# Six kinds of small VectorE operations moved to ScalarE, with new order tables, in an attention-and-SwiGLU kernel

## The chip, the cores and the metric

The kernel runs on one core of a Trainium2 chip. The metric is the device time of one execution in microseconds (us), as the median of several runs. A difference of about 0.2% (3.2 us here) is the least that such a measurement can tell from no change.

Five engines work side by side, each on its own queue and strictly in the queue's order: TensorE (PE, with its weight loads shown as PEld), VectorE (DVE), ScalarE (ACT), GpSimd (POOL) and SyncE (SP), which issues nearly all DMAs.

## The reference

Four batches of 12416 tokens with 128 channels pass through two attentions and a gated feed-forward network:

```python
scale = 1.0 / np.sqrt(C)
I = np.broadcast_to(inducing[None], (B, m, C))      # m = 32 inducing points
def mab(q, kv):
    s = scale * (q @ kv.transpose(0, 2, 1))
    s = s - s.max(-1, keepdims=True)
    a = np.exp(s)
    a /= a.sum(-1, keepdims=True) + 1e-09
    return a @ kv
h = mab(I, x)                 # 32 rows per batch
x = mab(x, h).reshape(B * S, D)
rms = np.sqrt(np.mean(x * x, axis=-1, keepdims=True) + 1e-06)
xn = x / rms * rms_g
g, val = xn @ w_gate, xn @ w_val          # 128 -> 1536
out = (g / (1 + np.exp(-g))) * val @ w_out    # 1536 -> 128
```

## The kernel before

**Units and slots.** A batch is cut into 25 units of up to 512 tokens (20 of 512, 4 of 480, 1 of 256), and each unit's 1536 hidden channels into 12 blocks of 128. One block of one unit is a slot, so there are 300 slots in a batch and 1200 in all. A slot (`slot`, L739) makes the gate product g (L742), its SiLU on ScalarE (L750), the value product v (L753), and silu times v on VectorE (L759). The slot's result is then multiplied by its block of `w_out` and added up over the unit's 12 blocks in the PSUM tile `acc`.

**Two ways to multiply by `w_out`.** A *plain* slot multiplies in float32 (`project`, L679): one matmul in the program, two records in the trace. A *split* slot (`three`, L718) first takes its block apart into parts, and then runs three faster float32r matmuls (`project3`, L695: lines L700, L702 and L679). There are two kinds of split: "sums" takes one ScalarE operation (L724), one VectorE (L725) and one GpSimd (L734); "differences" takes two ScalarE (L728, L733) and two GpSimd operations (L729, L734). A letter for each slot says which: s, d, or a dot for plain.

**The folded attention.** The second attention's 32 weights per token are the moving operand of the g and v products; h is folded into the weights once per batch, as the stacks `sg` and `sv`. So while batch b's slots run, batch b+1's first attention is worked out between them: `scores1`, `max1` to `max3`, `exp1_of`, `turn_e`, `sum_h`, `fold_l`, `divide`, `turn_h`, `square_h`, then `fetch`, `stack` and `place` for the stacks, and `scores2`, `row_max`, `sub_max`, `exp2` for the second attention's weights. Within batch b, `seam` (L496) scales each set's weights by the RMS factor and splits them (`turn_a` to `split`), and `gather` (L550) copies them by DMA into the tile `a`, which the g and v products of a unit read.

**What sets the order.** Everything is written out by hand and runs in program order on each engine. Tables inside the kernel hold the order: `letters` (the kind of each slot), `places` (the slot at which each step of attention and seam is issued), `ordered` (the points within each slot at which the output products are issued, "p" for a plain and "t" for a split one), and `banks`, `workers` and `holders` (which of 5 PSUM banks, 3 working tiles and 9 result tiles each use takes). In `steps` (L1117) of each slot the waiting second halves of splits come first, then the steps placed there, with products between them.

**Lines that the change touches.** All belong to the attention of a batch: `sum_h` L394 (first copy of the sum out of PSUM), `divide` L406 (division by the row sum, from SBUF to SBUF in batches 1 to 3), `turn_h` L413 (hT out of PSUM), `scale_h` L419 (hg = hT times the RMS gain, from SBUF to SBUF), `square_h` L431 (four 32x32 blocks of the Gram matrix), and `stack` L469 (the upper half of the stack out of PSUM). For batch 0 this part runs before the first slot. For batches 1 to 3 it lies in slots 146 to 227 of the batch before.

Of the kernel before, what the change touches and what calls it, by code (L numbers as in the profile page):

```python
# [9 lines left out]
F32 = mybir.dt.float32  # L10
# [8 lines left out]
P = 128  # L19
# [4 lines left out]
def kernel(  # L24
# [279 lines left out]
    def attention(b, load_next):  # L304
# [73 lines left out]
        def sum_h(*sets):  # L378
# [12 lines left out]
            if b and sets[0]:  # L391
                nc.vector.tensor_tensor(out=hl[:, 0:C], in0=hl[:, 0:C], in1=ps[:, 0:C], op=ALU.add)
            elif b:
                nc.vector.tensor_copy(out=hl[:, 0:C], in_=ps[:, 0:C])  # L394
# [9 lines left out]
        def divide():  # L404
            st["hn"] = st["hl"][:, 0:C]
            nc.vector.tensor_scalar_mul(out=st["hn"], in0=st["hn"] if b else st["ps"][:, 0:C], scalar1=st["rl"][:])  # L406

        def turn_h():

            ps = bank()  # L410
            nc.tensor.matmul(ps[:, 0:P], st["hn"], fold[:].rearrange("p q m -> p (q m)"), start=True, stop=True)
            hT = st["hT"] = once.tile([P, P], F32, name="hT")
            nc.vector.tensor_copy(out=hT[:], in_=ps[:, 0:P])  # L413
            if b:
                scale_h()

        def scale_h():
            hg = st["hg"] = once.tile([P, P], F32, name="hg")
            nc.vector.tensor_scalar_mul(out=hg[:], in0=st["hT"][:], scalar1=gam)  # L419

        def square_h():
# [6 lines left out]
            for q in range(R):  # L428
                to, of_ = gram[b][ts(q, m), ts(q, m)], ps[ts(q, m), 0:m]
                if b:  # L430
                    nc.vector.tensor_scalar(out=to, in0=of_, scalar1=1.0 / C, scalar2=1e-6, op0=ALU.mult, op1=ALU.add)  # L431
                else:
                    nc.scalar.activation(to, of_, AF.Copy, bias=1e-6, scale=1.0 / C)
# [27 lines left out]
        def stack(i):  # L461
# [7 lines left out]
            nc.vector.tensor_copy(out=hi[rows, :], in_=ps[rows, :])  # L469
# [503 lines left out]
    def given(b, k, u, j):  # L973
# [4 lines left out]
        ..........................dss.sdd...ss.sd.dsss..s.dss.dsds..sdsdsd...s..dsdd.sd..s..sd..sdsssd..ss.d  # L978
        sssdsd..d.ssdd.ss...ssssdsdsds....s..ds.sd..ssssssdsss..sdsdsd.sss..dss.ssddss...sssd.sssd..sdd.s.sd
        sd..s.sssdddss..sss.sssdss..ssssds.d.s..ssssd.ssss....s..dd.sd..s.ss.dssss..s.ssd...ss..ssdssssddd..  # L980
        """,
        """
        d..sdsd.ds..s..sd.ssds..ss..dsdssd...ssdssds.s..dsssd.sssd..sssd.s.dsd..dds.sd.dsd..ss..s.sssd..ssds
        sd.sds..sdsdsss.d...sss.sdssdd..s....d..dd..ssssssdssd..ssssssd.ss..sdsssssdss..sss.dssdsd..ssdsssss
        sd..sdds.ssssd..sss.s.sdsd..ss.s.ssssd...sssd.dsds....ss.sds.s..ss.dss.sds...ssss.sdss..ssd...ddds..
        """,
        """
        sd.sdd.sss.....dss.dsd..ssssdd.ssd..dss.sssdds...sssssdd.d..dsd...ssss..sdd.sssd.s..sds.dsssss..ssss
        dssd.s..d..dsssssd..sssdsdd.dd....s.s..dsd..sssdssdsss..sdssssss.s..dssdssssss..dsss.dsdss..ssssdssd
        sd..sssddsss.s..sssss.ssds..ssss.dsd.s..ssssssdsds....s..d.dd...ssssssssd...sss.s.ssss....ssdsddsd..  # L990
        """,
        """
        sd..d.ssssssds....ss.ssss.sssdds.dss.s..ssssdsss.ss.s.dsss.sssd...ssd..sss.sssssdssssss.ssds..ssss.s
        d.dssssssds..s.s.s.sssssd.ds.ss.sssssd.sss.ss.sssdds..sd.ssssds..ss.sss.ssd.ssss..sssssd.ss.sss.sd.s
        sds.ssssss.ss.sssd.ss..dss.sss.ssss.s.sssssssds..dsssss.ssdd..ss.ssss.sd.s..ssdssd.d.ssss.ssd....d..
# [5 lines left out]
        20 16 20 21 21 22 21 21 23 24 24 25 24 24 26 27 26 27 27 27 28 28 29 30 31 32 32 32 33 33 35 34 35 37 36 39   # L1001
        39 43 41 43 47 47 47 48 51 51 51 54 57 58 58 60 62 61 62 62 63 66 64 69 65 70 72 69 75 73 73 77 74 77 80 78 
        85 81 82 85 85 89 85 89 90 92 94 96 97 97 100 100 104 103 105 105 108 105 102 110 106 105 114 111 115 112 
        121 124 116 129 124 132 127 132 134 135 136 136 142 146 147 148 151 157 158 160 161 163 162 163 165 165 168 
        160 171 171 172 174 175 180 180 183 191 195 198 198 198 193 198 203 209 195 196 211 212 197 202 216 218 219 
        201 204 201 215 203 213 205 215 221 220 225 215 221 223 225 228 235 227 228 240 240 233 236 245 246 239 240 
        250 245 251 251 254 254 255 256 257 256 256 256 256 263 257 256 269 264 273 273 269 274 277 275 278 281 281 
        284 287 293 299 
        """,
        """  # L1010
        0 0 6 12 8 16 18 16 18 24 25 24 26 24 27 28 34 30 36 34 31 36 37 40 42 45 48 54 48 48 54 57 60 60 62 64 56 
        65 68 66 68 69 69 70 70 71 72 74 78 76 79 81 82 84 99 88 90 91 97 105 103 111 105 112 108 112 102 113 110 
        110 112 116 117 126 129 124 132 126 133 134 135 136 140 142 146 147 148 146 151 153 160 161 162 162 162 164 
        165 170 160 162 169 172 174 175 180 180 180 189 193 194 198 203 192 204 204 205 195 201 209 210 202 198 210 
        211 211 205 202 206 214 213 206 216 215 218 220 221 216 221 225 227 224 225 227 227 239 240 233 233 246 246 
        239 245 247 245 253 251 254 254 255 256 257 256 256 256 256 263 265 268 269 267 272 273 270 275 278 275 282 
        281 285 288 287 293 299 
        """,
        """
        0 0 6 12 5 11 18 11 18 12 15 21 29 24 26 29 34 30 36 32 32 36 36 37 42 46 48 51 48 49 54 57 57 60 66 60 52   # L1020
        61 55 66 56 67 62 67 72 74 72 79 74 81 75 82 75 84 91 86 86 96 97 101 103 108 103 110 108 111 109 111 112 
        112 117 120 119 124 129 120 132 128 133 134 135 136 142 143 146 147 148 147 158 151 160 161 157 162 157 160 
        161 164 162 168 169 169 174 175 174 180 180 188 195 196 198 204 199 206 206 210 202 211 210 212 197 205 212 
        216 216 207 213 207 213 209 215 211 220 216 221 216 226 228 226 234 225 234 239 236 240 247 240 248 250 254 
        254 255 256 255 255 256 257 258 256 260 261 261 273 273 279 282 285 287 
        """,
        """
        2 4 6 4 10 13 15 15 19 30 33 52 62 62 65 67 69 75 79 101 108 110 113 114 121 125 129 148 153 154 157 165 165 
        172 180 196 202 202 204 214 214 219 227 244 250 250 259 261 263 276 277 
# [3 lines left out]
        ;;;,p;,pp;;,pp;;,pp;;,pp;;;,pp,,,p;;,p;;;,p;;;p;,p;;,p;;,p;;;,pp;,pp;,pp;,tt;,tp,t;;,p;;,tp;;,tp;;,pp;;,tt;,t;  # L1033
        ;,pp;,t;;,pt;;,tt;;,t;,pp;;,tt;;,tt;,tp;;,t;,t;;;t,pp;,tt;;,tt;,t;,p;;,t;;,p;,pt;,pp;;;,tt;;,tp;;,tp;;,t;,tp;;
        ,t;,p;;,t;,tt;;,p;,tt;,tp;;,tp;,t;;;,tt;,pt;;,t;;t,t;;p,t;;;t,t;,p;t;,tp;;,tt;,p;;,tp;,t;;,tp;;,p;,tt;;t;,tp;;
        ,t;,p;;,tt;,pt;,pt;,tp;;,p;p;t,p;,p;,t;;,t;;,t;;,tp;;,tt;;,t;,tt;,tp;;,t;;,tt;,,t;,pt;;,t;;,t;,tt;;t,p;;,tp;,p
        t;;,t;,,p;,t;,tt;;,tt;,p;,,,tp;;;,tt;,t;,pt;;,tp;;,tp;,t;;,tt;;;,t;,tp;;,,t;,tt;,pp;;,t;,t;,tt;,p;;,t;;,pp;,t;
        ,t;,t;,t;,t;;;,t;,t;,tp;;,tp;,t;,t;,tp;,t;,t;,tp;,t;;,p;,t;,t;,pt;,t;;,t;;,tt;;,t;;,tp;;,tp;,t;;,t;,t;,t;,pt;;
        ,p;;,tt;,tt;,pp;,pp;;,tp;;p,p;;p,t;;,p;;,tt;;,pt;;,tt;;,tp;,t;;,tt;,tp;;,t;;,pp;;;t,tp;;,t;,p;,t;;,pt;;,tp;,t;
        ,t;,pt;,t;,t;,t;;,tp;,tp;;,tp;,t;;,pp;;,t;,tp;,t;;,t;,p;;,t;;,t;,t;;,tt;,pt;,p;;,tt;,pt;;,tp;;,pp;;,t;,t;,p;,t  # L1040
        p;,t;;,t;;,tt;;p;,tp;,p;,t;;,tt;;,tt;;,pt;,tp;,t;,pt;;;,t;t,t;;t,tp;;,tt;;;t,p;;,t;,tt;;;,tt;;,pt;;,t;,pp;;,tp
        ;;,pp;;,tp;,tt;;,tp;;,tp;;,t;,p;;,tp;,t;,p;,tt;;,tt;;,tt;;;,tp;;,tt;;;t,tt;;,pt;,t;;,tp;,t;,p;,tt;;,tp;;,t;;;t
        ;,t;,tp;;,p;,tp;;,t;,tt;;,t;,pt;;,tt;,pt;,pp;,tp;;,pp;,t;;,pp;,t;;,p;;,t;;,tp;;,tt;;,t;,tt;;,tt;;,t;,tp;;,tp;;
        ,t;;,tt;,tt;,tt;;,p;;,tp;,tp;;,tp;;,t;,t;,t;,tt;,,,tp;;,tt;;,t;,p;;,tt;,tp;,t;,t;,t;;;t,,t;;,t;,pt;,t;,t;,t;,t
        ;,t;;,tt;,p;;,t;,tp;;,t;,t;,t;,t;,tp;,tt;;,t;;,tp;;,pp;,t;,pt;;,tp;,t;;;,t;,t;,tp;;,tp;;,t;,tt;;p,t;;,tt;;,t;;
        ,p;,t;;,t;,tt;;,pt;;,p;;,tp;,tp;,tp;,tp;;,p;t,pp;,t;,t;;,p;;,t;,t;,t;,pt;;,tp;;,t;,tt;,p;;,t;,t;,t;,p;,p;,p;,t
        t;;,tt;;,pt;,p;,p;,t;,t;;,t;;,p;,tt;;,pt;;p,pt;;,t;,p;,tt;,pp;;,t;,t;;t,p;,t;;,t;,t;;,tp;;;t,p;,p;,tp;,t;,tp;;
        ,t;;,tp;;,tp;,pt;;,t;,tt;;,tp;;,tt;;,tp;;,t;;,pp;,tt;,t;;,t;,tt;,p;;,tp;;t;,t;,p,t;;,t;,tt;,t;;t,p;;,tp;,tp;;,
# [117 lines left out]
```

## Time and profile before

| | |
|---|---|
| median of 3 runs | 1592.77 us (1592.2 to 1593.33) |
| profiled execution | 1593.12 us, of it span 1591.2 us |
| granted TensorE clock | 1.00 |
| ACT busy in the span | 1300.7 us (82%), 2473 instructions |
| POOL busy | 1442.6 us (91%), 1167 instructions |
| DMA | 112.57 MB, mean 71 GB/s |

The first slot starts at about 54 us; until then the first batch's attention runs, with gaps on every engine. From 100 us on PE is shown busy nearly all the time, DVE and POOL for some 93% and 95% of it, ACT for some 83%. Matmul ends in the trace are modelled, so a matmul that waits can look busy; the spacing from start to start is the surer measure.

### The profile page before, as it was taken

Reading aid. Unit: us, or ns where it says so; the run is one execution under the profiler, and the core shown is the slowest. Engines: PE = TensorE matmul, PEld = TensorE weight load, DVE = VectorE, ACT = ScalarE, POOL = GpSimd, SP = SyncE. Lnnn points to the kernel's source line nnn. Section 1 sums busy time; section 2 is a strip of 40 time slices with the busy share of each in tenths; the row PEclk is TensorE's granted clock in tenths of the full one; section 3 lists DMA queues with packets and bytes.
Section 4 is the critical chain, followed back from the end, with each engine's and each line's share of the span. In section 5 each row is a group of like instructions: output and inputs, shape, how many; then the busy total and the mean of one; then the engine's idle time right before and its main releaser. Section 6 shows DMA issues by size and latency. Waiting matters only on the chain.

```text
span 1591.2 us, 26159 instructions
## 1 busy us (share of the span) xinstructions
PE 1577.6 (99%) x7191; PEld 1108.7 (70%) x7191; DVE 1458.6 (92%) x2531; ACT 1300.7 (82%) x2473; POOL 1442.6 (91%) x1167
## 2 busy tenths in 40 slices
PE   8999999999999999999999999999999999999998
PEld 7556667766776666766677667676667677777776
DVE  4899998999989998999998999899998999999997
ACT  4587888778888889877888888977798888888887
POOL 1289998999899998999899999999999999999998
PEclk9999999999999999999999999999999999999999
DMA  7455534434454141634335314362221112221211
GB/s 267 93 76 87 86 66 92 105 84 82 68 83 73 30 96 31 134 85 80 67 63 91 57 36 88 63 131 69 52 39 36 32 32 40 38 38 34 38 37 29
DMA packets 389186, 112.57 MB, mean 71 GB/s; under 512 B 365072, under 2 KB 369712, under 8 KB 386480
## 3 DMA queue, kind: packets, MB, share of 16 engines
q1 hardware_dynamic: 388304, 110.82, 35.3%
q8 instruction: 57, 0.93, 0.3%
q14 instruction: 89, 0.73, 0.2%
q10 hardware_dynamic: 736, 0.08, 0.0%
HBM read 53.95 MB, written 27.00 MB: 51 GB/s over the span
## 4 chain that ended last, share of the span: by engine, by line
PE 94%; DVE 1%; DMA 0%; issue 0%; POOL 0%; ACT 0%; SPq 0%; POOLq 0%; DVEq 0%; ACTq 0%
PE acc L679 31%; PE gv L742 18%; PE gv L753 17%; PE u L702 11%; PE u L700 11%; PE gv L336 3%; PE gv L512 1%; PE gv L390 1%; DMA a<-lo 0%; PE gv L466 0%; PE gv L480 0%; DVE u L759 0%; POOL lo L546 0%; SPq L558 0%; DVE gv L759 0%
## 5 line engine op out<-in xcount | busy, mean ns | idle before, releaser
L750 ACT ACTIVATE silu<-gv 128x512 f32<-128x512 f32 (+2 forms) x1186 | 684.7, 587 | 158.8 <-PE gv L742 147.8
L734 POOL TENSOR_TENSOR xn<-xn,xn 128x512 fp32r<-128x512 f32 (+2 forms) x620 | 767.1, 1257 | 46.1 <-DVE xn L725 20.2
L753 PE MATMUL gv<-a,sv 128*128 128x512 f32 (+2 forms) x1188 | 569.1, 480 | 0.7 <-DVE u L759 0.4
L742 PE MATMUL gv<-a,sg 128*128 128x512 f32 (+2 forms) x1188 | 483.8, 408 | 1.8 <-DMA a<-lo 1.3
L759 DVE TENSOR_TENSOR u<-silu,gv 128x512 f32<-128x512 f32 (+2 forms) x595 | 387.1, 655 | 46.7 <-PE gv L753 22.3
L759 DVE TENSOR_TENSOR gv<-silu,gv 128x512 f32<-128x512 f32 (+2 forms) x591 | 395.9, 674 | 35.5 <-PE gv L753 17.9
L679 PE MATMUL acc<-u,wo 128*128 128x512 f32 (+2 forms) x778 | 379.8, 577 | 0.0
L742 PEld LDWEIGHTS gv<-a,sg 128*128 128x128 f32 x1188 | 223.4, 188 | 150.9 <-issue 33.1
L724 ACT ACTIVATE xn<-gv 128x512 fp32r<-128x512 f32 (+2 forms) x460 | 271.0, 589 | 54.1 <-DVE gv L759 38.4
L725 DVE SCALAR_TENSOR_TENSOR xn<-xn,gv 128x512 fp32r<-128x512 f32 (+2 forms) x460 | 304.0, 661 | 6.9 <-ACT xn L724 4.0
L753 PEld LDWEIGHTS gv<-a,sv 128*128 128x128 f32 x1188 | 223.6, 188 | 110.0 <-issue 25.9
L700 PE MATMUL u<-xn,xn 128*128 128x512 f32 (+2 forms) x599 | 243.9, 407 | 0.0
L679 PE MATMUL acc<-xn,more 128*128 128x512 f32 (+2 forms) x599 | 231.2, 386 | 0.0
L729 POOL TENSOR_TENSOR xn<-u,xn 128x512 fp32r<-128x512 f32 (+2 forms) x160 | 199.0, 1244 | 8.1 <-ACT xn L728 8.1
L679 PEld LDWEIGHTS acc<-u,wo 128*128 128x128 f32 x778 | 145.0, 188 | 43.0 <-issue 16.3
L700 PEld LDWEIGHTS u<-xn,xn 128*128 128x128 f32 x599 | 112.6, 188 | 31.3 <-issue 7.3
L734 POOL TENSOR_TENSOR sg<-sg 128x512 fp32r<-128x512 f32 (+1 forms) x96 | 123.4, 1286 | 6.6 <-DVE sg L725 1.8
L679 PEld LDWEIGHTS acc<-xn,more 128*128 128x128 f32 x599 | 112.5, 188 | 23.5 <-POOL xn L734 0.4
L734 POOL TENSOR_TENSOR sv<-sv 128x512 fp32r<-128x512 f32 (+1 forms) x95 | 122.6, 1291 | 5.4 <-PE acc L679 1.0
L702 PE MATMUL u<-xn,more 128*128 128x512 f32 (+2 forms) x309 | 119.6, 387 | 0.0
L702 PE MATMUL u<-xn,xn 128*128 128x512 f32 (+2 forms) x290 | 111.6, 385 | 0.0
L728 ACT ACTIVATE xn<-u 128x512 fp32r<-128x512 f32 (+2 forms) x160 | 98.1, 613 | 15.3 <-DVE u L759 10.7
(203 smaller groups left out, 1933.4 us busy)
## 6 DMA issues: line engine op xcount, KB each, us to landing
out_dram<-o SPq DMA_DIRECT2D x320, 64.0 KB, 2.0
xT<-in_x_dram SPq DMA_DIRECT2D x60, 256.0 KB, 4.4
xn<-in_x_dram SPq DMA_DIRECT2D x60, 256.0 KB, 5.3
a<-hi SPq DMA_DIRECT2D x156, 64.0 KB, 2.0
a<-lo SPq DMA_DIRECT2D x156, 64.0 KB, 2.0
xn<-in_x_dram SPq DMA_DIRECT2D x5, 1024.0 KB, 10.2
xn<-w SPq DMA_DIRECT2D x18, 256.0 KB, 3.2
out_dram<-o SPq DMA_DIRECT2D x64, 60.0 KB, 2.0
```

Of the source, the lines that this page charges most:

```text
L679: nc.tensor.matmul(acc[:, 0:T], lhsT, rhs, start=st["left"] == NJ, stop=st["left"] == 1)
L700: nc.tensor.matmul(ups[:, 0:T], weight_of(0, j), hi, start=st["k"] == nk, stop=False)
L702: nc.tensor.matmul(ups[:, 0:T], weight_of(1, j), lo, start=False, stop=not st["k"])
L724: nc.scalar.activation(hi, v, AF.Copy, scale=(1.0 - 2.0 ** -13) * 2.0 ** -12)
L725: nc.vector.scalar_tensor_tensor(out=lo, in0=hi.bitcast(F32), scalar=-4096.0, in1=v, op0=ALU.mult, op1=ALU.add)
L728: nc.scalar.activation(d, v, AF.Copy, scale=1.0 - 2.0 ** -13)
L729: nc.gpsimd.tensor_tensor(out=lo, in0=v, in1=d.bitcast(F32), op=ALU.subtract)
L734: nc.gpsimd.tensor_tensor(out=d, in0=hi.bitcast(F32), in1=lo.bitcast(F32), op=ALU.subtract)
L742: nc.tensor.matmul(g[:, 0:T], sg[:, ts(j, P)], a[:, 0:T], start=True, stop=True)
L750: nc.scalar.activation(sl[:, 0:T], g[:, 0:T], AF.Silu)
L753: nc.tensor.matmul(v[:, 0:T], sv[:, ts(j, P)], a[:, 0:T], start=True, stop=True)
L759: nc.vector.tensor_tensor(out=t[:, 0:T], in0=sl[:, 0:T], in1=v[:, 0:T], op=ALU.mult)
```

## The change

Six kinds of operations of batches 1 to 3 go from VectorE to ScalarE: the first copy of the sum (`sum_h`), the division (`divide`), hT, hg (now taken from PSUM beside hT, and no longer from hT), the four Gram blocks (`square_h`), and the upper half of the stacks (`stack`). Batch 0 keeps its own: its division, hT and hg stay on VectorE. The one line of `stack` serves batches 1 to 3 alone.

```diff
             elif b:
-                nc.vector.tensor_copy(out=hl[:, 0:C], in_=ps[:, 0:C])
+                nc.scalar.copy(out=hl[:, 0:C], in_=ps[:, 0:C])
...
             st["hn"] = st["hl"][:, 0:C]
-            nc.vector.tensor_scalar_mul(out=st["hn"], in0=st["hn"] if b else st["ps"][:, 0:C], scalar1=st["rl"][:])
+            if b:
+                nc.scalar.activation(st["hn"], st["hn"], AF.Copy, scale=st["rl"][:])
+            else:
+                nc.vector.tensor_scalar_mul(out=st["hn"], in0=st["ps"][:, 0:C], scalar1=st["rl"][:])
...
             hT = st["hT"] = once.tile([P, P], F32, name="hT")
-            nc.vector.tensor_copy(out=hT[:], in_=ps[:, 0:P])
             if b:
-                scale_h()
+                nc.scalar.copy(out=hT[:], in_=ps[:, 0:P])
+                hg = st["hg"] = once.tile([P, P], F32, name="hg")
+                nc.scalar.activation(hg[:], ps[:, 0:P], AF.Copy, scale=gam)
+            else:
+                nc.vector.tensor_copy(out=hT[:], in_=ps[:, 0:P])
...
                 to, of_ = gram[b][ts(q, m), ts(q, m)], ps[ts(q, m), 0:m]
-                if b:
-                    nc.vector.tensor_scalar(out=to, in0=of_, scalar1=1.0 / C, scalar2=1e-6, op0=ALU.mult, op1=ALU.add)
-                else:
-                    nc.scalar.activation(to, of_, AF.Copy, bias=1e-6, scale=1.0 / C)
+                nc.scalar.activation(to, of_, AF.Copy, bias=1e-6, scale=1.0 / C)
...
-            nc.vector.tensor_copy(out=hi[rows, :], in_=ps[rows, :])
+            nc.scalar.copy(out=hi[rows, :], in_=ps[rows, :])
```

All tables are replaced: `letters`, `places`, `ordered`, `banks`, `workers` and `holders`, for all four batches. The first line of letters of the second batch, as an example:

```diff
-        d..sdsd.ds..s..sd.ssds..ss..dsdssd...ssdssds.s..dsssd.sssd..sssd.s.dsd..dds.sd.dsd..ss..s.sssd..ssds
+        d...dsssss..dssssdsd.s..dd.sd.sd.s..ssd.ss.dss..sds.sddsss..sdd...ds.d..ssss.d.dsd...ssssdsssd..ssd.
```

Counted over the tables, batch by batch:

| | before | after |
|---|---|---|
| "sums" slots | 125, 140, 148, 180 = 593 | 132, 142, 147, 181 = 602 |
| "differences" slots | 58, 62, 60, 38 = 218 | 53, 61, 56, 37 = 207 |
| plain slots | 117, 98, 92, 82 = 389 | 115, 97, 97, 82 = 391 |
| split slots of 512, 480, 256 tokens | 656, 125, 30 | 658, 122, 29 |

The steps of the attention are placed anew as well. Three kinds of matmuls of the attention work on quarters of the array, 128 rows by 32 columns each: the scores (`scores`, L336, for `scores1` and `scores2`), the stacks (L466) and the sums (L390). A burst is what stands together of these on TensorE's queue, with no other matmul between. Written as slot numbers within the batch, with S for one set's scores and K for one stack, the bursts are these (the three bursts of sums in each of batches 0 to 2, at slots 146, 160 and 174, are the same in both):

| batch | before | after |
|---|---|---|
| 0 | 16 SS, 21 S, 24 S, 26 S, 27 S, 51 S, 62 S, 77 S, 89 S, 100 S, 110 S, 116 S, 193 S, 198 K, 202 S, 211 K, 213 S, 215 S, 228 S, 236 S, 240 S | 16 SS, 24 SSSS, 54 S, 65 S, 77 S, 89 S, 96 S, 116 SS, 198 K, 208 SSK, 215 SS, 230 S, 239 SS |
| 1 | 34 S, 54 S, 62 S, 74 S, 99 S, 111 S, 116 S, 192 S, 194 K, 198 S, 206 S, 209 K, 216 S, 227 S, 233 S, 245 S | 35 S, 54 S, 66 S, 87 SS, 118 SS, 198 K, 204 SSSK, 216 S, 233 SS, 244 S |
| 2 | 32 S, 51 S, 66 S, 79 S, 91 S, 108 S, 120 S, 196 K, 199 S, 205 S, 210 K, 215 S, 216 S, 225 S, 236 S, 240 S | 35 S, 50 S, 66 S, 93 SS, 120 SS, 197 SK, 203 SK, 219 SS, 229 SSS |

That is 53 bursts of scores and stacks before and 32 after, with the same 54 sets of scores and stacks in them. Each set and each stack takes a PSUM bank of its own, out of five that it shares with the g and v products.

The last split of weights before batch 2 begins stood at slot 289 of batch 1 and now stands at 285; the one of batch 0's second set moves from slot 43 to 44. The DMAs, their number and their sizes are the same: 1079 issues on SP in both.

## Prediction

> **What bounds the kernel now.** I read the page first: engine shares, then the chain of waits.
>
> ```profile
> PE 1577.6 (99%) x7191; PEld 1108.7 (70%) x7191; DVE 1458.6 (92%) x2531; ACT 1300.7 (82%) x2473; POOL 1442.6 (91%) x1167
> ...
> PE 94%; DVE 1%; DMA 0%; issue 0%; POOL 0%; ACT 0%; SPq 0%; POOLq 0%; DVEq 0%; ACTq 0%
> PE acc L679 31%; PE gv L742 18%; PE gv L753 17%; PE u L702 11%; PE u L700 11%; PE gv L336 3%; PE gv L512 1%; PE gv L390 1%; DMA a<-lo 0%; PE gv L466 0%; PE gv L480 0%; DVE u L759 0%; POOL lo L546 0%; SPq L558 0%; DVE gv L759 0%
> ```
>
> TensorE carries the chain, and the other engines are near it. So the time is TensorE's work plus what it loses. Its start-to-start spacing gives prices: 0.23 us for an undisturbed 512-wide g, v or split product, and 0.86 for a plain one ("acc L679 x4", two of them, is 1.72 in the chain). A split costs 0.69, so it saves 0.17; by the same rows 0.15 at 480 and 0.08 at 256.
>
> Next I looked at what surrounds the quarter-array bursts. The timeline of TensorE, columns start and length, has a burst with one set of scores and one with two:
>
> ```profile
> 1108.03 0.40 PE L753 MATMUL gv<-a,sv 128*128 128x512 f32 x1
> 1108.35 1.06 PE L336 MATMUL gv<-xT,hT 128*32 128x512 f32 x8
> 1109.35 0.50 PE L742 MATMUL gv<-a,sg 128*128 128x512 f32 x1
> 1109.69 0.39 PE L700 MATMUL u<-xn,xn 128*128 128x512 f32 x1
> ```
>
> ```profile
> 78.60 0.40 PE L753 MATMUL gv<-a,sv 128*128 128x512 f32 x1
> 78.92 1.92 PE L336 MATMUL gv<-xT,hT 128*32 128x512 f32 x16
> 80.78 0.50 PE L742 MATMUL gv<-a,sg 128*128 128x512 f32 x1
> 81.11 0.40 PE L753 MATMUL gv<-a,sv 128*128 128x512 f32 x1
> ```
>
> From the matmul before the burst to the second one after it: 1.66 us with one set, 2.51 with two. A second set costs 0.86 (1.86 - 1.00). The first costs 1.66 less two products of 0.23, that is 1.20. So entering and leaving the quarter form costs 0.34 per burst, whatever is in it. The stacks (L466, 0.99) and the 480- and 64-wide scores show the same excess, the 256-wide ones 0.31.
>
> Last, VectorE at the third head (batch 3's hT and hg), in the chain and in the rows of two lines (minimum/median/maximum ns), with GpSimd's timeline row:
>
> ```profile
> 1087.16 0.20 DVE hT L413
> 1087.37 0.02 issue
> 1087.39 0.03 DVE hg L419
> 1087.42 1.23 issue
> 1088.65 0.69 DVE gv L759
> ```
>
> ```profile
> L419 DVE TENSOR_SCALAR hg<-hT,columns x4: 286/726/1340, 39.7 to 1087.4; 128x128 f32<-128x128 f32 x4
> L406 DVE TENSOR_SCALAR hl<-hl,rl x3: 617/902/1166, 309.0 to 1077.0; 128x128 f32<-128x128 f32 x3
> ```
>
> ```profile
> 1086.10 2.55 POOL L734 TENSOR_TENSOR xn<-xn,xn 128x512 fp32r<-128x512 f32 x2
> ```
>
> hg, alone 0.286 us, takes 1.34 and ends at 1088.73; GpSimd's row is two operations that end at 1088.65. The SBUF-to-SBUF operation stood until GpSimd's ended, with VectorE's queue behind it.
>
> **The change part by part.**
>
> *Bursts.* The new order has 32 bursts of scores and stacks where there were 53, with the same sets in them. 21 x 0.34 = **-7.1 us**, on TensorE itself. Nothing hides it, since TensorE is the chain. The Trainium skill (TensorEngine Tiling (Array Packing), Key Properties) says that changing the tiling mode drains TensorE; it gives no price, the rows do. The same page (PSUM Bottleneck) speaks against the change: tiling does not speed up emptying PSUM. The longest burst, three scores and a stack, takes 4 x 0.86 + 0.34 = 3.8 us and four of the five banks. Emptying them takes VectorE three transposes of 0.70 and a subtraction of 0.69, 2.8 us. By the rule this blocks the next g and v; by the rows it fits in the burst, if VectorE has nothing else queued.
>
> *Starved engines in longer bursts.* During a burst no g or v comes. Around the sums' bursts of 1.9 to 2.1 us at 255, 274 and 294 us ScalarE sits idle up to 0.97 us before the next SiLU, and the chain stays on TensorE. So 2.1 us are covered. Four bursts are longer: batch 0's SSSS (512, 512, 480 and 256 wide, 3.3 us) and SSK (2.9), batch 1's SSSK (3.8), batch 2's SSS (512, 480 and 256, 2.4). The excess is 1.2 + 0.8 + 1.7 + 0.3 = 4.0 us. Bounds 0 and +4.0; I take **+1.5**, nearer to nothing, because the covered rows are the nearest.
>
> *Slots.* Splits go from 656, 125, 30 (by width) to 658, 122, 29: -2 x 0.17 + 3 x 0.15 + 1 x 0.08 = **+0.2**. The tables do not buy speed with more splits.
>
> *VectorE.* Removed in batches 1 to 3: three copies of the sum and three hT (0.283 each, 1.7), three divisions (2.7), three hg (2.8; the two long ones 1.15 and 1.34), twelve Gram blocks of 0.186 (2.2), six upper halves of 0.68 (4.1): 13.5 us. Sums slots rise by 8 at 512 and 2 at 256 and fall by 1 at 480; their L725 of 0.68, 0.42 and 0.64 adds 5.6. Net -7.9.
>
> *ScalarE.* Twelve Gram blocks at 0.188 (its own row, L433) 2.3; six halves at 0.58 (L481) 3.5; twelve 128x128 operations, for which no row exists. Between 0.188 at 32 columns and 0.60 at 512 a straight line gives 0.27; six of them read their scale from a tile, which costs 0.08 going by the exponentials with and without a tile bias (1.144 against 1.060): 3.7. Splits: sums +8, -1, +2 (512, 480, 256 wide) at 0.60, 0.57, 0.38, differences -6, -2, -3 with two operations each: -7.3. Net +2.2.
>
> *GpSimd.* Thirteen operations fewer: 4 x 1.30 + 5 x 1.225 + 4 x 0.74 = -14.3 us.
>
> *What that is worth.* Only where TensorE loses time. I summed, over TensorE's records, each start less the previous start and the undisturbed spacing: 35.3 us in 100 to 1250 us, but 2.7 in 1250 to 1550, where no attention runs. In three stretches with the moved operations (300 to 375, 690 to 765, 1075 to 1150) it is 13.1. Of that 4.4 are edges of their 22 bursts (0.2 of each 0.34 counts here) and 2.3 the level of the late stretch; 6.4 are left. VectorE is at 93 to 95% there, ScalarE at 76 to 78%:
>
> ```profile
> 300.00:375.00 75.00, 75.00 (x315) 48.87 (x313) 70.06 (x119) 58.22 (x109) 71.29 (x57) 1.00 0.37 75
> 1075.00:1150.00 75.00, 74.49 (x315) 48.86 (x314) 71.24 (x121) 56.91 (x107) 70.26 (x56) 1.00 0.28 63
> ```
>
> (The pairs are PE, PEld, DVE, ACT, POOL.) About half of the waits of weight loads there and elsewhere end on ScalarE (silu 39.1 us) and half on VectorE (u, gv and L725, 53), so I take half of 6.4: **-3.2**, bounds 0 and -6.4. A rule speaks against moving them: the skill's Perfetto Trace Analysis (Optimizing Scalar/DVE Operations) says that VectorE is faster where it has a performance mode. By that rule and the unblocked 0.286, the six SBUF operations lose 6 x (0.35 - 0.286) = 0.4 us; by the blocked rows they free 5.5 us of VectorE for 2.1 of ScalarE. The rows decide. What is late next is ScalarE, whose queue puts four Gram blocks (0.75 us) ahead of a SiLU; without the slack that the 76% shows this would cost 0.75 three times.
>
> *New waits.* The lower half of a stack (VectorE) now waits for the upper on ScalarE, with silu-times-v products behind it; the division on ScalarE waits for the reciprocal on VectorE, with SiLUs behind. The division stands one, five and eight slots after the reciprocal, so its wait is over by then. The other is six times up to one ScalarE operation of 0.6: bounds 0 and 3.6, counted in the +1.5 above.
>
> *Seams.* At 839.5 us TensorE waits for the first weights of batch 2: the split ends at 834.6, the copy lands at 839.4, and 0.67 us are lost. Its split moves four slots earlier: **-0.7**. The similar loss of 0.79 at 124.5 keeps its place within a slot: 0, at worst +1.3 for the one slot. DMAs are the same in number and size.
>
> Sum: -7.1 + 1.5 + 0.2 - 3.2 - 0.7 = **-9.3 us**. Against the profiled execution of 1593.12 that is 1583.8, against the median of 1592.77 **1583.5**.
>
> **The rivals.**
>
> *Slower: banks starve after merged bursts.* The place is the first g or v after each of the 15 bursts that became longer. In the burst VectorE and ScalarE run dry; then they must empty several banks and catch up, at 95% load. Against it stands the two-set burst above, with no wait behind it; for it the 95%. Each would cost a transpose and a queue place, 0.7 to 1.3 us. The other terms are -10.8, so it decides from 10.8 / 15 = 0.72 each; at 1.0, 1592.8 - 10.8 + 15 = **1597**. Chance 10%.
>
> *No relief and dear bursts.* VectorE's relief lies in slack (0 for -3.2), and bursts take back 0.3 each: 1592.8 - 7.1 + 0.2 - 0.7 + 4.5 = **1589.7**. Chance 14%.
>
> *More is cleared.* The new order also takes the small losses elsewhere: 35.3 less 10.6 (level) less 11.2 (edges of 56 bursts) is 13.5, in place of 3.2, and no penalty. 1592.8 - 7.1 + 0.2 - 13.5 = 1572.4 is the end; half way, **1578**. Chance 14%.
>
> *The change does not do what it says.* Bursts adjacent in order may be apart in time when a bank is not free; then the saved entry is a wait of the same size. This is in the second rival.
>
> **How the numbers follow.** The forecast has 62%. Faster by over 0.2% (3.2 us): 61 + 14 + 7 = 82%; within 0.2%: 1 + 6 + 2 = 9%; slower 9%, about what a measurement can tell from no change being that 0.2%. The forecast's own bounds, all at their best, give -14.0 (1578.8); all at their worst (bursts +4.0, waits +3.6, no relief) 0.0 (1592.8). With the rivals, 8 in 10 lie in 1576.5 to 1592.
>
> **What would show it.** Scores in one run of 16, 24 or 32 records with 0.86 per set, and fewer 0.32 gaps before L336; hT and hg on ScalarE at about 0.27 and 0.35; no operation over 1 us on VectorE in the heads; no DMA piece near 839. It is wrong if g or v after merged bursts waits for VectorE, or if weight loads wait for ScalarE by much more than 39 us.

## The result, and the profile after

The changed kernel takes **1587.2 us** (median of 6 runs, 1585.81 to 1587.53) beside 1592.31 (1592.11 to 1593.33) for the kernel before: a ratio of 0.9965, 95% interval 0.9952 to 0.9978, or 5.1 us less. The forecast was 9.3 us less. The profiled execution took 1587.39 us, with a span of 1585.5; the span before was 1591.2.

In later comparisons the executions of the kernel before fell into two groups, near 1592.2 and 1597.4 us, for a reason that no trace here shows, and its medians there (1593.87, 1592.46 and 1592.48) mix them; so differences in microseconds below are taken from the lower group, 1592.2.

The first lines of the page of after are the busy times, and the chain's shares by engine and by line. (Lines of code past L404 stand three further down than before.)

```profile
PE 1571.7 (99%) x7189; PEld 1112.7 (70%) x7189; DVE 1453.4 (92%) x2510; ACT 1300.9 (82%) x2490; POOL 1428.2 (90%) x1154
...
PE 94%; DVE 1%; SPq 1%; issue 0%; ACT 0%; DMA 0%; DVEq 0%; ACTq 0%
PE acc L682 31%; PE gv L745 18%; PE gv L756 17%; PE u L705 11%; PE u L703 11%; PE gv L336 2%; PE gv L515 1%; PE gv L390 1%; SPq L478 0%; DVE u L762 0%; PE gv L483 0%; PE gv L469 0%; DVE gv L762 0%; ACT silu L753 0%; DVE o L693 0%
```

GpSimd lost 14.4 us of busy time, VectorE 5.2, and ScalarE gained 0.2; the forecast had 14.3, 7.9 and 2.2. TensorE still carries the chain with 94%. New is "SPq 1%", with L478: SP's queue at the DMAs that place the stacks' halves. It was not in the forecast.

The moved operations have rows of their own on ScalarE now (minimum/median/maximum ns):

```profile
L419 ACT ACTIVATE hg<-gv,columns x3: 373/378/415, 322.5 to 1093.1; 128x128 f32<-128x128 f32 x3
```

```profile
L472 ACT CAST whi<-gv x6: 577/582/583, 326.1 to 1103.6; 96x512 fp32r<-96x512 f32 x6
```

hg costs 0.378 us, an upper half 0.582, and a 128x128 copy 0.268 by its own row, where the forecast took 0.35, 0.58 and 0.27. hg ranges from 0.373 to 0.415; on VectorE, in before, it ranged from 0.286 to 1.340.

**Where the time went.** TensorE makes the same kinds of slots in both kernels, so the start of the k-th of the 1200 SiLUs says how far a kernel has come. The table gives that start less the one of the kernel before, in us, from one profiled execution each (of e3_ops_only, one of 1597.52 us). Two executions of after differ in it by up to 0.8, of which 0.5 is there at the first slot already; other rows start between -0.1 and -0.9. Where the tables differ, so does the order of products within a slot, and neighbouring slots can differ by over 1 us. So differences of about 1 us are at the limit of this table. The heads, where the attention of the next batch is finished, lie in slots 140 to 230, 440 to 530 and 740 to 830. The lower rows are experiments, told below.

| kernel | 140 | 230 | 440 | 530 | 740 | 830 | last | sum of the three heads |
|---|---|---|---|---|---|---|---|---|
| after | -2.6 | -4.1 | -2.9 | -2.0 | -2.7 | -6.0 | -6.0 | -3.9 |
| e3_ops_only | -0.4 | +0.1 | +4.5 | +4.8 | +4.1 | +4.2 | +4.3 | +0.9 |
| e4_tables_only | -3.4 | -2.2 | -1.4 | +3.9 | +2.9 | +2.8 | +1.8 | +6.4 |
| e5_own | -3.3 | -5.8 | -4.9 | -5.8 | -6.7 | -11.0 | -11.1 | -7.7 |
| e6_before_own | -0.5 | -0.5 | -0.4 | -0.5 | -0.7 | -0.7 | -0.7 | -0.1 |
| e8_tables_own | -2.8 | -2.3 | -1.4 | +1.2 | +0.2 | -0.6 | -1.5 | +2.3 |
| e12_sbuf_back | -2.7 | -2.3 | -1.4 | +0.4 | -0.6 | -1.5 | -1.1 | +1.3 |

In after the heads of batches 0 and 2 gain, 1.5 and 3.3 us, and the one of batch 1 loses 0.9. There the timeline of TensorE (start, length, and in brackets the idle time and what ended it) shows the longest burst, three scores and a stack:

```profile
717.79 1.06 PE L336 MATMUL gv<-xT,hT 128*32 128x512 f32 x8
719.48 0.63 PE L469 MATMUL gv<-xn,hg 128*32 128x512 f32 x3 [0.62 <-DVE z L521]
...
722.19 0.49 PE L745 MATMUL gv<-a,sg 128*128 128x512 f32 x1
723.30 0.50 PE L756 MATMUL gv<-a,sv 128*128 128x512 f32 x1 [0.62 <-DVE wlo L473]
```

The stack starts 1.69 us after the scores that take 0.86, so 0.8 us are lost in the burst. The value product starts 1.11 after the gate product, where 0.34 is usual on leaving a burst: nearly 0.8 more. VectorE's timeline at the same time tells why:

```profile
715.11 1.42 DVE L762 TENSOR_TENSOR u<-silu,gv 128x512 f32<-128x512 f32 x2
718.77 0.66 DVE L521 TENSOR_TENSOR z<-gv,eT 128x480 f32<-128x480 f32 x1 [2.24 <-DMA sg<-whi]
...
722.56 0.69 DVE L473 TENSOR_TENSOR wlo<-gv,whi 96x512 fp32r<-96x512 f32 x1 [0.63 <-DMA sg<-wlo]
```

VectorE stands 2.24 us at `z` and then 0.63 at `wlo`, each until a DMA out of `whi` or `wlo` has landed. (`z` is the result of a step of the seam, and takes a working tile as well.) The chain shows what those DMAs take, start and length of each piece:

```profile
719.78 0.59 SPq L478
720.37 0.04 issue
720.41 2.03 DMA sg<-wlo
```

SP issues one in 0.63 us, and one lands 2.03 us after its issue began. Each stack has 12 of them, six out of `whi` and then six out of `wlo`. So `whi` is held for 5 x 0.63 + 2.03 = 5.2 us from the first issue and `wlo` for 9.0 (two working tiles of three), and longer where SP issues other DMAs in between (here four stores of results, 713.4 to 715.4 us).

The two stacks of a batch stand 13 to 15 slots apart in before (198 and 211, 194 and 209, 196 and 210), but 10, 6 and 6 in after (198 and 208, 198 and 204, 197 and 203). In batch 1 the second stack's `wlo` takes the tile of the first one's. But the longer wait, and the only one in the other two heads, is that of `z`. The table `workers` gives it the tile of a stack's `whi` in every head of both kernels. It is issued 3, 12 and 11 slots behind that stack in before (201, 206 and 207), and 4, 4 and 7 in after (202, 202 and 210). VectorE's timeline of after in the heads of batches 0 and 2:

```profile
333.44 0.66 DVE L521 TENSOR_TENSOR z<-gv,eT 128x480 f32<-128x480 f32 x1 [1.77 <-PE acc L682]
...
1114.79 0.66 DVE L521 TENSOR_TENSOR z<-gv,eT 128x480 f32<-128x480 f32 x1 [1.13 <-PE gv L745]
```

These two waits are put down to TensorE, but the last DMA out of that `whi` lands at 333.17 and 1114.57 us, 0.2 to 0.3 before `z` starts. In before, batch 0 has `z` as near to the stack, but VectorE comes to it at 335.20 us, 0.5 after the landing.

### The profile page after: what moved, and what is told of

Read it like the earlier page. It is cut to its first block, busy times and chain, and to the rows that moved or that the text cites. A ratio compares the mean times of both kernels' runs of the same rounds, so it can differ in the third digit from the quotient of the medians.

```text
span 1585.5 us, 26129 instructions
## 1 busy us (share of the span) xinstructions
PE 1571.7 (99%) x7189; PEld 1112.7 (70%) x7189; DVE 1453.4 (92%) x2510; ACT 1300.9 (82%) x2490; POOL 1428.2 (90%) x1154
## 4 chain that ended last, share of the span: by engine, by line
PE 94%; DVE 1%; SPq 1%; issue 0%; ACT 0%; DMA 0%; DVEq 0%; ACTq 0%
PE acc L682 31%; PE gv L745 18%; PE gv L756 17%; PE u L705 11%; PE u L703 11%; PE gv L336 2%; PE gv L515 1%; PE gv L390 1%; SPq L478 0%; DVE u L762 0%; PE gv L483 0%; PE gv L469 0%; DVE gv L762 0%; ACT silu L753 0%; DVE o L693 0%
## 5 line engine op out<-in xcount | busy, mean ns | idle before, releaser
L762 DVE TENSOR_TENSOR gv<-silu,gv 128x512 f32<-128x512 f32 (+2 forms) x598 | 400.5, 675 | 38.7 <-PE gv L756 19.5
L762 DVE TENSOR_TENSOR u<-silu,gv 128x512 f32<-128x512 f32 (+2 forms) x588 | 382.4, 656 | 37.4 <-PE gv L756 17.8
L727 ACT ACTIVATE xn<-gv 128x512 fp32r<-128x512 f32 (+2 forms) x468 | 275.9, 590 | 54.0 <-DVE gv L762 38.4
L728 DVE SCALAR_TENSOR_TENSOR xn<-xn,gv 128x512 fp32r<-128x512 f32 (+2 forms) x468 | 309.8, 662 | 8.1 <-ACT xn L727 2.9
L732 POOL TENSOR_TENSOR xn<-u,xn 128x512 fp32r<-128x512 f32 (+2 forms) x150 | 187.6, 1251 | 8.0 <-ACT xn L731 7.3
L705 PE MATMUL u<-xn,more 128*128 128x512 f32 (+2 forms) x300 | 115.9, 386 | 0.0
L731 ACT ACTIVATE xn<-u 128x512 fp32r<-128x512 f32 (+2 forms) x150 | 92.4, 616 | 10.7 <-DVE u L762 5.0
```

The costliest lines, as they stand in the source:

```text
L705: nc.tensor.matmul(ups[:, 0:T], weight_of(1, j), lo, start=False, stop=not st["k"])
L727: nc.scalar.activation(hi, v, AF.Copy, scale=(1.0 - 2.0 ** -13) * 2.0 ** -12)
L728: nc.vector.scalar_tensor_tensor(out=lo, in0=hi.bitcast(F32), scalar=-4096.0, in1=v, op0=ALU.mult, op1=ALU.add)
L731: nc.scalar.activation(d, v, AF.Copy, scale=1.0 - 2.0 ** -13)
L732: nc.gpsimd.tensor_tensor(out=lo, in0=v, in1=d.bitcast(F32), op=ALU.subtract)
L762: nc.vector.tensor_tensor(out=t[:, 0:T], in0=sl[:, 0:T], in1=v[:, 0:T], op=ALU.mult)
```

## The experiments

### Are the edges of a burst real?

The rival said that merged bursts only turn the saved entries into waits. **e1_apart** puts one 128x128·128x1 product, into the set's own bank, ahead of each of the 21 sets that were merged; so each set is entered and left as in before, at the price of a small product. **e2_front** issues the same 21 products ahead of the bursts and lets the bursts be. Its counts, one for each set, are those of e1 moved to the burst's first set.

```diff
+    extra = [int(c) for c in "00000000000111000000100110100100001010011100100000101010101011"]
+    def full_form(ps):
+        for _ in range(extra.pop(0)):
+            nc.tensor.matmul(ps[:, 0:1], fold[:].rearrange("p q m -> p (q m)"), ones[:], start=True, stop=True)
...
             ps = bank()
+            full_form(ps)
```

> The kernel after, with a one-column full-array product put before each of the 21 sets of scores or stacks that the new order merged into a burst: the order and all else stay, but each merged set enters the quarter form anew. The theory that entering and leaving costs 0.34 us per burst expects 1587.2 + 21 x 0.34 + 21 x 0.13 for the product itself = 1597 (range 1594 to 1600). The rival, that merging does nothing by itself and the gain came from moved operations or better tables, expects only the products' own 2.7 us or less: 1587 to 1590.

> The control to the bursts pulled apart (1592.5): the same 21 one-column products, put together before the first set of the merged bursts, where the array is in its full form anyway. Each should cost 0.10 to 0.13 us, so 1586.5 or 1587.2 + 2 to 2.7 = 1588.5 to 1590 if TensorE's work sets the time, and less where TensorE waits anyway. The difference to the bursts pulled apart is what 21 entries into the quarter form cost in this order: 7.1 us if all of it counts, 3 to 5 if a part falls into waits.

Measured: e1_apart 1592.52 us (1592.11 to 1593.36; ratio 0.9985, 0.9977 to 0.9993) and e2_front 1587.59 (1587.21 to 1587.92; 0.9957, 0.994 to 0.9974). So e1_apart lies between what the theory and the rival expected of it, and gives back the whole gain of the change. The small products as such cost 0.4 us; the edges cost 4.9 us more, 0.23 for each of 21. The two ran on different chips, and two measurements of the changed kernel differ by 0.7 us, so the 4.9 is good to about that. TensorE's timeline of e1_apart:

```profile
87.60 1.06 PE L343 MATMUL gv<-xT,hT 128*32 128x512 f32 x8
88.59 0.38 PE L296 MATMUL gv<-columns,fold 128*128 128x1 f32 x2
88.90 1.06 PE L343 MATMUL gv<-xT,hT 128*32 128x512 f32 x8
```

Sets start 1.30 us apart, against 0.86 inside a burst. In e2_front's trace a single small product adds 0.11 us (0.23 after the product before it and 0.21 ahead of the burst, where 0.33 is usual without it), and one of three in a row 0.19. That leaves 0.25 to 0.33 for leaving and entering, beside the forecast's 0.34. That the kernel loses 0.23 and not 0.34 can come from this price, or from edges that fall into time that TensorE waits in any case. The latter is seen in batch 1's longest burst: pulled apart, its three edges and products are 3 x 0.44 = 1.3 us, but from the first scores to the value product it takes 5.95 us in e1_apart (720.81 to 726.76) and 5.51 in after.

### Moved operations and tables, each alone

**e3_ops_only** is before with the moved operations and its own tables; **e4_tables_only** has the new tables with the six kinds back on VectorE.

```diff
 # e3_ops_only, against before: the code of the change, tables kept
-                nc.vector.tensor_copy(out=hl[:, 0:C], in_=ps[:, 0:C])
+                nc.scalar.copy(out=hl[:, 0:C], in_=ps[:, 0:C])
...
 # e4_tables_only, against after: the six kinds as in before, new tables kept
-            nc.scalar.copy(out=hi[rows, :], in_=ps[rows, :])
+            nc.vector.tensor_copy(out=hi[rows, :], in_=ps[rows, :])
...
```

> The kernel before with its own tables, and the six kinds of operations on ScalarE. The prediction's term for VectorE's relief expects -3.2 us against before (1589.1; bounds -6.4 and 0, and the heads' operations of over 1 us gone from VectorE). The rival, that the relief lies in slack because TensorE is fed anyway, expects no change, within 1 us of 1592.3.

> The kernel after with its new tables, and the six kinds of operations back on VectorE. If the tables and their bursts are the gain, it stands within 1.5 us of after (1587 to 1589). If the move of the operations carries the gain, it returns towards before (1590 or more).

Measured: e3_ops_only 1595.38 us (1592.01 to 1598.79; ratio 1.0002, 0.9988 to 1.0015), or 1593.2 as the median of its 7 executions below 1594. e4_tables_only 1595.85 (1594.62 to 1596.96; 1.0007, 0.9997 to 1.0017).

So neither part gains anything alone. With before's tables the move is worth nothing (1592.2 to 1593.2); with the new tables it is worth 8.6 us (1595.85 to 1587.2). The two parts are not terms that add up: the new order costs more than it saves unless the operations leave VectorE. The table above shows where. From the first slot to slot 140 e4_tables_only gains as much as after (2.5 us each); in the three heads it loses 6.4 us where after gains 3.9. In VectorE's timeline of e4_tables_only, in the head of batch 1, both kinds of stop stand together:

```profile
709.87 1.26 DVE L419 TENSOR_SCALAR hg<-hT,columns 128x128 f32<-128x128 f32 x1
...
724.36 0.66 DVE L518 TENSOR_TENSOR z<-gv,eT 128x480 f32<-128x480 f32 x1 [2.67 <-DMA sg<-whi]
```

### Which of the six kinds?

**e9_halves_back** returns only the upper halves to VectorE, **e10_others_back** the five other kinds, and **e12_sbuf_back** only the division and hg, the two that go from SBUF to SBUF (its hT stays on ScalarE).

```diff
 # e9_halves_back
-            nc.scalar.copy(out=hi[rows, :], in_=ps[rows, :])
+            nc.vector.tensor_copy(out=hi[rows, :], in_=ps[rows, :])
 # e12_sbuf_back (e10_others_back: these, hT, the sum's copy and the Gram blocks)
-            if b:
-                nc.scalar.activation(st["hn"], st["hn"], AF.Copy, scale=st["rl"][:])
-            else:
-                nc.vector.tensor_scalar_mul(out=st["hn"], in0=st["ps"][:, 0:C], scalar1=st["rl"][:])
+            nc.vector.tensor_scalar_mul(out=st["hn"], in0=st["hn"] if b else st["ps"][:, 0:C], scalar1=st["rl"][:])
...
-                nc.scalar.activation(hg[:], ps[:, 0:P], AF.Copy, scale=gam)
+                scale_h()
```

> The kernel after with only the upper halves of the stacks back on VectorE (6 x 0.68 us). Of the 9 us that putting all six kinds back costs, a theory of plain load (4.1 of 13.5 us of VectorE's time) gives this kind 2.7: 1589.5. The theory that the waits of SBUF-to-SBUF operations for GpSimd carry it gives it little: 1586.5 to 1588.

> The kernel after with all kinds but the upper halves back on VectorE (9.4 of 13.5 us). Plain load: + 6.2, 1593. Waits for GpSimd: nearly all of the 9 us, 1594 to 1596.

> The kernel after with only the two kinds from SBUF to SBUF back on VectorE, the division and hg (six operations, 5.5 us with their waits, 1.7 without). The theory of waits for GpSimd expects most of what all kinds cost: 1590 to 1594. Plain load by their unblocked length (1.7 of some 10 us) expects 1587 to 1588.

Measured: e9_halves_back 1588.54 us (ratio 0.9965, 0.9955 to 0.9976), e10_others_back 1592.24 (0.9988, 0.998 to 0.9996), e12_sbuf_back 1591.99 (0.9991, 0.9983 to 0.9998). Against 1587.2 the halves are worth 1.3 us (not clear of noise) and the five others 5.0, of which 4.8 belong to the division and hg. Together that is 6.3 of the 8.6 us; 2.3 come only when all go back at once. So neither theory holds throughout: e9_halves_back lies between the two and e10_others_back below both, nearest to plain load; e12_sbuf_back alone is where the waits for GpSimd put it. The division and hg are six operations, and 1.7 us of work if nothing blocks them. In e12_sbuf_back they take up to five times their least time:

```profile
L421 DVE TENSOR_SCALAR hg<-hT,columns x4: 286/676/1401, 39.6 to 1096.7; 128x128 f32<-128x128 f32 x4
```

Its chain in the first head, and the timeline of GpSimd there:

```profile
318.00 1.38 DVE hl L406
319.37 0.14 DVE gv L758
...
319.89 0.69 DVE xn L724
...
320.62 0.49 PE gv L741
```

```profile
318.02 1.27 POOL L733 TENSOR_TENSOR xn<-xn,xn 128x512 fp32r<-128x512 f32 x1
```

The division starts within 0.02 us of GpSimd's operation and ends 0.09 after it; two VectorE operations stand behind it, and TensorE's next gate product behind those. The Trainium skill (SBUF — State Buffer, Who interferes with whom) says that a VectorE operation of this kind (`tensor_scalar`) can run in a mode that takes a pair of ports which it shares with GpSimd; whichever of the two issues first holds the pair for its whole instruction, and the other blocks. 1.38 and 1.27 agree with it; no run here shows the mode itself, and starts 0.02 us apart do not tell which came first. In after's chain the same stretch is TensorE's alone.

In the third head of e12_sbuf_back hg takes 1.40 us and TensorE's first stack waits for it:

```profile
1098.19 0.63 PE L465 MATMUL gv<-xn,hg 128*32 128x512 f32 x3 [1.85 <-DVE hg L421]
```

With 0.22 in the first head this is 2.1 of the 4.8 us. A part may come from the way the edit splits the work: hg on VectorE now waits for hT on ScalarE, as in neither kernel. In e4_tables_only, e8_tables_own and e10_others_back, with hT on VectorE too, the stack waits 0.72 us for hg, once; in before and after never.

### The working tiles of the stacks

If the placing DMAs hold the working tiles, halves that lie elsewhere must free VectorE. **e5_own** is after with the halves written into the fourth and first quarters of the tile that holds the stack's fetched weights: the fourth is unused, and the first has been read by then. **e6_before_own** does the same to before, and **e8_tables_own** to e4_tables_only. Tables and all DMAs stay.

```diff
-            home = xnp.tile([P, 4, 512], F32, name=f"xn{i}")
+            home = st["home", i] = xnp.tile([P, 4, 512], F32, name=f"xn{i}")
...
-            hi, lo = st["halves", i] = [worker([P, 512], F32R, n) for n in ("whi", "wlo")]
+            del works[:2]
+            hi, lo = st["halves", i] = [st["home", i][:, c, :].bitcast(F32R) for c in (NC, 0)]
```

> The kernel after, with the two halves of each stack not in the three working tiles but in the two parts of the fetched weights' own tile that are free by then; nothing else changes. The theory that the stacks now stand so near to each other that VectorE's z and lower half wait for the placing DMAs of the stack before (SP issues them 0.59 us apart) expects the waits at 717 to 724 and 1115 us gone: -2.9 us of lost TensorE time against after, 1584.3 (range 1583.5 to 1585.5). The rival, that PSUM banks starve after the burst of three scores and a stack whatever the working tiles do, expects the same time as after, within 0.7 us of 1587.2, with the wait on VectorE's transposes left.

> The kernel before with only the halves of the stacks moved out of the working tiles. In before the two stacks stand 13 to 15 slots apart, and no wait for a placing DMA is in its chain. The theory that the working tiles hurt only because the new order puts the stacks 4 to 10 slots apart expects no change against before (within 0.7 us of 1592.3). The rival, that freeing the working tiles is a gain by itself in any order, expects 3 to 5 us less, 1587 to 1589.

> The new tables, the halves out of the working tiles, and the six kinds of operations on VectorE. The new tables with the operations on VectorE ran at 1595.9. If what they lost there is the same wait for the placing DMAs, made worse, this one comes to 1584 or less, near the version with the operations on ScalarE (1582.3). If the operations themselves delay VectorE in the heads, it stays 4 us or more above that version: 1586 to 1592.

Measured: e5_own **1582.32 us** (1582.1 to 1582.5; ratio 0.9919, 0.9904 to 0.9934), faster than both kernels; e6_before_own 1592.46 (0.9996, 0.9984 to 1.0009), no different from before; e8_tables_own 1591.64 (0.9986, 0.9979 to 0.9994). On the chip that ran these, **e11_after_again**, the changed kernel once more, took 1586.5 (1586.25 to 1587.15; 0.9953, 0.9937 to 0.997).

> The kernel after once more, on the chip that also runs the next three, as their reference: 1587.2 us expected, within 1.5.

So the wait for the working tiles costs the changed kernel 4.2 us there (4.9 against the first median), and the kernel before nothing. That is more than the 2.9 us expected, which counted two heads. By the starts of the SiLUs e5_own gains on e11_after_again in three steps, where `z` waits in after: 1.2, 2.0 and 1.1 us. The longest burst in e5_own, on TensorE:

```profile
715.88 1.06 PE L336 MATMUL gv<-xT,hT 128*32 128x512 f32 x8
716.76 0.61 PE L469 MATMUL gv<-xn,hg 128*32 128x512 f32 x3
...
719.44 0.50 PE L746 MATMUL gv<-a,sg 128*128 128x512 f32 x1
719.78 0.40 PE L757 MATMUL gv<-a,sv 128*128 128x512 f32 x1
```

From the first scores to the value product it is 3.90 us, 5.51 in after. Both long waits are gone, and no engine that runs dry in a burst of four sets keeps TensorE waiting behind it. e8_tables_own and e5_own differ by the six kinds alone, by 9.3 us: the value of the move in this order, with the working tiles out of play. Freeing the tiles is worth 4.2 us with the six kinds on VectorE, too (1595.85 to 1591.64). So in the new order these two effects add up, and the tiles are not why the move is worth more there.

### One operation more

**e7_best** takes e5_own and moves to ScalarE the small 1x128 operation of `max2` (L353), the one SBUF-to-SBUF operation of this part that the change left on VectorE.

```diff
-            nc.vector.tensor_scalar_mul(out=row4, in0=row[:].unsqueeze(1).to_broadcast((1, R, m)), scalar1=-SCALE)
+            wide_row = row[:].unsqueeze(1).to_broadcast((1, R, m))
+            if b:
+                nc.scalar.activation(row4, wide_row, AF.Copy, scale=-SCALE)
+            else:
+                nc.vector.tensor_scalar_mul(out=row4, in0=wide_row, scalar1=-SCALE)
```

> The kernel after with the halves out of the working tiles (1582.3 us), and the small SBUF-to-SBUF product of max2 (1x128) of batches 1 to 3 on ScalarE. On VectorE it stood 0.42 to 1.27 us in the profiles of after and 4.25 us in one of a run at 1597.5. Theory: it stands until GpSimd leaves a gap, so the move takes away at most 1 us of VectorE's queue and makes the time steadier: 1581.5 to 1582.5. The rival, that the wait is covered, expects 1582.3 and no change.

Measured: 1583.74 us (1583.64 to 1584.49; ratio 0.9937, 0.9922 to 0.9952), 1.4 us more than e5_own, outside both expectations, but less than 0.2%. ScalarE takes it in 0.31, but stands 1.3 us in all for VectorE's `row` ahead of it, with SiLUs behind. So this one does not help; that the wait is what costs more than the relief is worth was not tested by itself.

## Why the prediction was right in its sign and half right in its size

- **What bounds the kernel.** Right: TensorE carries 94% of the chain in both.
- **Bursts, -7.1.** Right in mechanism: after has 32 bursts in its trace, a set more costs 0.86, and an edge 0.25 to 0.33 (e1_apart, e2_front). Mis-sized as an effect on the end: 21 edges come to 4.9 us (e1_apart less e2_front), not 7.1.
- **Starved engines in longer bursts, +1.5.** For the longest burst the mechanism fell: e5_own shows it with no wait of TensorE in it, though VectorE is as busy over the span (1452.8 us against 1453.4). The forecast's sign of being wrong, a value product after a merged burst that waits for VectorE, did come in after (723.30 us), but from elsewhere, next point.
- **"DMAs are the same in number and size": the step that failed.** Number and size are, but the sum priced the moved stacks without their 12 placing DMAs on SP's queue, which move with them. In all three heads `z` is to be written into the tile of a `whi` that SP (0.63 us an issue, 2.03 to land) is still reading, and in batch 1 the second `wlo` into that of the first. That costs 4.2 to 4.9 us. The forecast missed by 4.2; without the wait e5_own lies at 1582.3, beside a forecast of 1583.5. The two agree, but not term by term, as the next point shows.
- **VectorE's relief, -3.2.** Wrong as a term of its own. In before's order it is nothing (e3_ops_only), as the second rival said; in the new order it is 8.6 to 9.3, above the bound of 6.4. The bound was read from what TensorE loses in before's order, so it could not hold what the operations would cost in another. Of the six kinds the two from SBUF to SBUF carry 4.8 us (e12_sbuf_back). The mechanism, that they stand until GpSimd's operation ends, was the forecast's. Why the new order bears them worse is shown only in part: `turn_h` stands 7, 5 and 8 slots ahead of the first stack in before (191 and 198, 189 and 194, 188 and 196) and 2, 3 and 1 in after (196 and 198, 195 and 198, 196 and 197), so the stack follows hg more closely, and in the runs with hg on VectorE TensorE waits for it, 0.72 to 2.1 us. The rest is open.
- **The sum.** That it came out with the right sign and half the size is in part luck. The terms of the order come to -6.1 us (-7.1 + 1.5 + 0.2 - 0.7); the new order alone measures +3.6 (e4_tables_only; -0.6 with the working tiles free, e8_tables_own). The term of the move is -3.2; in the new order it measures -8.6. Two errors of 9.7 and 5.4 us went opposite ways.
- **A rule against the move.** The rows did decide, as the forecast chose: SBUF operations on ScalarE do not lose 0.4 us but gain 4.8 in this order. The forecast gave half of what that section of the Trainium skill (Perfetto Trace Analysis, Optimizing Scalar/DVE Operations) says: it goes on that moving some work to ScalarE may make sense where VectorE is saturated, and with VectorE 92% busy this half agrees with the runs in the new order.
- **Seam at 839.5, -0.7.** The chain of after is TensorE's alone there, with no DMA in it. The size is not shown: e3_ops_only and e6_before_own, whose order there is before's, get past this place 0.7 and 0.4 us quicker than before's profiled execution, too.
- **Slots, +0.2.** Not tested alone. After slot 830, where hardly any attention is left, after neither gains nor loses beyond the table's limit (-6.0 and -6.0).
- **Rivals.** Of the slower one the effect came, a wait after the merged stacks, but by other means: tiles held by DMAs, not banks, and at three places, not fifteen. The second rival's number, 1589.7, is nearer to the measured 1587.2 than the forecast's 1583.5, but not by its means: starved banks did not make the bursts dear, and "no relief" holds in before's order alone.

How large the interaction of order and operations is has been measured; how the new order brings it about stays open but for the waits for hg.

## What to carry to other kernels

A step that is moved takes its DMAs along: count their issues on the queue, and look at which tile they read and who writes that tile next. When a schedule and an engine assignment change together, try each alone before adding their gains, since here one was worth 0 in the old order and 9 us in the new. On VectorE, such an SBUF-to-SBUF operation beside a busy GpSimd can cost as long as GpSimd's instruction and not its own length (1.40 us here for an hg that takes 0.29 alone), so it is a candidate to move; but e7_best, with 1.4 us more, shows no gain from the next such move.

## What was unexpected of the hardware

In the profiled execution of e3_ops_only (1597.52 us) the small 1x128 operation of `max2` took 4.25 us on VectorE:

```profile
615.66 4.25 DVE L353 TENSOR_SCALAR hg<-row 1x128 f32<-1x128 f32 x1
```

GpSimd's timeline beside it:

```profile
615.06 1.29 POOL L737 TENSOR_TENSOR xn<-xn,xn 128x512 fp32r<-128x512 f32 x1
616.32 1.28 POOL L732 TENSOR_TENSOR xn<-u,xn 128x512 fp32r<-128x512 f32 x1
617.57 1.04 POOL L536 TENSOR_TENSOR sc<-sc,rs 128x512 f32<-128x512 f32 x1
618.58 1.25 POOL L737 TENSOR_TENSOR xn<-xn,xn 128x512 fp32r<-128x512 f32 x1
```

It did not wait for one instruction, as the section of the skill named above has it, but from within the first of four that followed each other without a gap to the end of the fourth. It ended at 619.91, within 0.1 us of that one, after which GpSimd stood idle for 1.42 us. In before's profiled execution the same line takes 0.6 to 0.9 in batches 1 to 3.

The stop cost TensorE more than idle time: no product started from 617.86 to 621.16 us, and then the granted clock was 0.50 for 3.4 us, with products 0.43 us apart in place of 0.23. A window of it (length; busy time of PE, PEld, DVE, ACT and POOL with counts; granted clock; DMA share and GB/s):

```profile
621.00:624.00 3.00, 2.84 (x6) 2.11 (x7) 3.00 (x6) 2.92 (x7) 2.75 (x3) 0.50 0.00 0
```

By the starts of the SiLUs the stop takes 3.4 us and the slow stretch another 1.0. In the table above this one event is the whole of e3_ops_only's loss: +4.5 at slot 440, and flat from there.
